# Moving weight conversions between steps: three doubled steps in the first feed-forward layer, two steps with none in the second

## The chip, the cores and the metric

One NeuronCore of a Trainium2 chip runs the whole program in one launch. The metric is the device time of that launch in microseconds (us). The engines are named as in the profile: PE multiplies matrices (PEld are its weight loads), DVE works elementwise, ACT evaluates functions and copies, POOL works elementwise too, and SP issues the DMAs.

## The reference

The program computes an attention with rotary embedding (2 batches, 8 heads, 576 positions, 64 per head) and passes its result, 1152 tokens of 512 features, through two feed-forward layers with 2048 hidden features:

```python
x = attention(q, k, v)                     # 1152 x 512
h = x @ moe_w_in;   g = where(h > 0, h, exp(min(h, 0)) - 1)       # first layer, ELU
x = g @ moe_w_out
h = x @ moe2_w_in;  g = h * tanh(softplus(h))                     # second layer, Mish
out = g @ moe2_w_out
```

The four weight matrices arrive as 64-bit floats, everything else as 32-bit floats.

## The kernel before, in words

**Products in three passes.** Every operand of a product is split into a high and a low part (`XH` and `XL` for activations entering a layer, two halves of a `g` tile for activations between the two products of a layer, and pairs such as `wi0h`, `wi0l` for weights), and the product is the sum high x high, high x low, low x high.

**Steps.** After attention the program is a sequence of 64 steps, numbered 0 to 63, one call of `step(n, late)` each. `half` is 32: steps 0 to 31 belong to the first layer, 32 to 63 to the second. A step first issues `g1_mm` (L199): 24 matmuls of 288 columns (L207) that make one 128 x 576 block of `h` in a PSUM tile `ps_s`, of which there are two until step 39. Then it issues the activation function of that block, and then one or two units of the second product that are due: in the first layer `g2_first` (24 matmuls of 288 columns, L752), in the second `g2_second` (12 matmuls of 512 columns, L781). Four of the first layer's second products are due only in steps 34, 35, 36 and 38; they complete the activations of batch 1 for the second layer, with `Y` added on DVE (L765), `XH` copied on ACT (L766) and `XL` subtracted on DVE (L767). The second layer's first product reads batch 1 from step 40 on.

**The activation functions.** In the first layer ACT runs L238, L239 and L240, DVE runs L241 and L242 (L242 is the last reader of `ps_s`), ACT copies the high part (L247) and DVE subtracts the low part (L251). In the second layer ACT reads `ps_s` twice (L708, L709; L709 is its last reader), DVE multiplies (L710), and for a batch of steps together ACT loads a table and runs L716, loads another and runs L722, after which DVE (L723, L730) and ACT (L729) finish the `g` tiles.

**Weight conversions.** There are 64 weight blocks ("jobs") of 128 x 512 numbers. `weight_stages` (L86) converts one from 64 to 32 bits and splits it: POOL multiplies (L96), DVE runs three operations (L100, L104, L108), ACT copies the high part (L125), POOL subtracts the low part (L128). Three buffers `raw` hold blocks that were loaded (L78, L83) and two buffers `wu` blocks under work. The generator yields between these, so that `advance(i)` does the next piece of the i-th of the two running jobs; `open_job` starts one (L96), `weight_part` opens jobs until two run and advances the first, `weight_job` calls it until one more job is done. Eight jobs are done during attention. Steps 4 to 30 do one job each: three pieces ahead of the activation function, the last piece (L125, L128) between L240 and L247. From step 31 on `weight_job` comes at the end of a step, once per step, and twice in step 36 (`XJ`). Jobs 40 to 43 are the blocks `wo0h`, `wo0l` that the first `g2_second` of step 39 multiplies with.

**Order.** In the first layer the order of every engine is the program's own. In the second layer (from step 32) that holds for ACT alone; the order on the other engines is chosen by the scheduler of the language from its own costs. Every engine works through its list in order.

Of the kernel before, what the change touches and what calls it, by code (L numbers as in the profile page):

```python
# [27 lines left out]
def kernel(  # L28
# [109 lines left out]
    def prefetch_weights():  # L138
        while loaded[0] < min(len(jobs), freed[0] + 3):
            load_weight(jobs[loaded[0]])  # L140
            loaded[0] += 1

    def open_job():
        prefetch_weights()
        running.append(weight_stages(jobs[opened[0]]))
        opened[0] += 1
        advance(-1)

    def advance(i):
        if next(running[i], True):  # L150
            running.pop(i)
            njob[0] += 1
# [21 lines left out]
    def weight_part():  # L174
        while len(running) < 2 and opened[0] < len(jobs):
            open_job()
        if running:
            advance(0)

    def weight_job():  # L180
        n = min(njob[0] + 1, len(jobs))
        while njob[0] < n:
            weight_part()
# [15 lines left out]
    def g1_mm(m, f, b):  # L199
        c = m * NF + f  # L200
        hi, lo = WI[c]
        o = ps_s()
        k = 0
        for cc in range(NC):
            for w, x in ((hi, XH), (hi, XL), (lo, XH)):
                for j in range(2):
                    nc.tensor.matmul(  # L207
                        o[:, j, :HS], lhsT=w[:, cc, :], rhs=x[:, b, cc, j * HS:j * HS + HS],
                        start=(k == 0), stop=(k == 3 * NC - 1),
                    )  # L210
                k += 1
        return o
# [22 lines left out]
    def elu(m, f, b, o):  # L235
        h = o[:, :, :HS]
        t, g = tmp("ta"), tmp("tb")
        nc.scalar.activation(out=v2(g), in_=h, func=AF.Relu, scale=-1.0)  # L238
        nc.scalar.activation(out=t, in_=g, func=AF.Exp, scale=-1.0)  # L239
        nc.scalar.activation(out=g, in_=g, func=AF.Tanh, scale=-0.5)  # L240
        nc.vector.scalar_tensor_tensor(out=g, in0=t, scalar=1.0, in1=g, op0=ALU.add, op1=ALU.mult)  # L241
        nc.vector.tensor_tensor(out=v2(g), in0=v2(g), in1=h, op=ALU.max)  # L242
        return m, f, b, g

    def elu_hi(m, f, b, g):
        gh, gl = galloc(m, f, b)
        nc.scalar.activation(out=gh, in_=g, func=AF.Copy)  # L247
        return g, gh, gl

    def elu_lo(g, gh, gl):  # L250
        nc.vector.tensor_tensor(out=gl, in0=g, in1=plain(gh), op=ALU.subtract)  # L251
# [438 lines left out]
    def moe(mp, early):  # L690
# [15 lines left out]
        def mish_a(n, m, f, b, o):  # L706
            t, s = tmp("ta"), tmp("tb")
            nc.scalar.activation(out=v2(t), in_=o[:, :, :HS], func=AF.Tanh, scale=0.5)  # L708
            nc.scalar.activation(out=v2(s), in_=o[:, :, :HS], func=AF.Silu)  # L709
            nc.vector.scalar_tensor_tensor(out=s, in0=t, scalar=-3.0, in1=s, op0=ALU.add, op1=ALU.mult)  # L710
            mst[n] = (m, f, b, t, s)

        def mish_b(ns):
            for n in ns:
                t = mst[n][3]
                nc.scalar.activation(out=t, in_=t, func=AF.Ln, scale=-NEAR_HALF, bias=half_col)  # L716

        def mish_c(ns):
            nc.scalar.preload_act_table_set("silu_and_others")
            for n in ns:  # L720
                m, f, b, t, s = mst[n]
                nc.scalar.activation(out=t, in_=t, func=AF.Tanh, scale=-1.0)  # L722
                nc.vector.scalar_tensor_tensor(out=s, in0=t, scalar=1.0, in1=s, op0=ALU.add, op1=ALU.mult)  # L723

        def mish_d(ns):
            for n in ns:
                m, f, b, t, s = mst.pop(n)
                gh, gl = galloc(m, f, b)
                nc.scalar.activation(out=gh, in_=s, func=AF.Copy, scale=-0.25)  # L729
                nc.vector.scalar_tensor_tensor(  # L730
                    out=gl, in0=s, scalar=-0.25, in1=plain(gh), op0=ALU.mult, op1=ALU.subtract
                )
                seam(m, f, b)
# [60 lines left out]
        blocks[-4:] = [(1, g, b) for g in range(NG - 2, NG) for b in range(NB)]  # L794
        g1_seq = [(m, g * GF + fi, b) for m, g, b in blocks for fi in range(GF)]
        half = len(g1_seq) // 2
        D1, D2, LATE, XJ = 1, 4, (3, 4, 5, 7), 4
        pend = []

        def run_g2(it):  # L800
            if it[0] == 0:
                g2_first(*it[1])
            else:
                g2_second(*it[1])
# [6 lines left out]
        def step(n, late):  # L811
            m, f, b = g1_seq[n]
            o = early.pop(n) if n in early else g1_mm(m, f, b)
            if late:
                mish_c(late)
            done, late = late, []
            if m == 0:
                for _ in range(3 if GF <= n < half - 1 else 0):
                    weight_part()
                if o is not None:  # L820
                    o = elu(m, f, b, o)
                if GF <= n < half - 1:
                    weight_part()
                if o is not None:
                    o = elu_hi(*o)
            else:
                mish_a(n, m, f, b, o)
                mish_d(done)
            if f % GF == GF - 1:
                g = f // GF  # L830
                if m == 0:
                    pend.extend((n + (D1 if n < half - 1 else LATE[e]), (0, (g, b, e))) for e in range(NC))
                else:
                    pend.extend((n + D2, (1, (g, t))) for t in TB[b])
            if n in batches:
                late = batches[n]
                mish_b(late)
            cnt = 2 if len(pend) > 5 or pend and pend[0][1][0] == 0 and n in (half - 2, half + 6) else 1
            while pend and cnt and pend[0][0] <= n:
                run_g2(pend.pop(0)[1])  # L840
                cnt -= 1
            if m == 0:
                if o is not None:
                    elu_lo(*o)
            for _ in range(0 if n < half - 1 else 1 + (n == half + XJ)):
                weight_job()
            return late

# [9 lines left out]
        with tc.manual_schedule():  # L858
            for n in range(half):
                step(n, [])  # L860
        with tc.manual_schedule(engines=MANUAL):
            late = []
            for n in range(half, 2 * half):
                if n == half + 7:
                    psum("ps_h")
                    s_more[0] = g_pool[0]
                    s_count[0] = 0
                late = step(n, late)
            mish_c(late)
            mish_d(late)  # L870
            while pend:
                run_g2(pend.pop(0)[1])
# [18 lines left out]
    with tc.tile_pool(name="mp", bufs=1, reuse_waits="tile") as mp:  # L891
        moe(mp, early)
# [54 lines left out]
```

## Time and profile before

| | us |
|---|---|
| median of 3 runs | 596.75 |
| lowest and highest of these | 593.58, 596.79 |
| the profiled execution's own time | 596.55 |
| its span in the trace | 594.8 |
| PE busy | 562.9 |
| DVE busy | 430.5 |
| ACT busy | 362.5 |
| POOL busy | 242.5 |

The span is what the trace covers; the execution's own time is 1.75 us longer. Busy times are sums over the whole span, so an engine with a small share can still be the one that is waited for in a short stretch. Times in rows are counted from the start of the span. In the rows, an entry in square brackets at the end gives the idle time of that engine just before the row and who ended it.

### The profile page before, as it was taken

How to read it: one execution, taken by the hardware profiler on the slowest of the kernel's cores; microseconds unless marked ns; L12 is line 12 of the kernel's file. 1: busy time of each engine (PE TensorE's matmuls, PEld its weight loads, DVE VectorE, ACT ScalarE, POOL GpSimd, SP SyncE). 2: the span in 40 equal slices, each digit the busy share in tenths (PEclk: the TensorE clock that was granted, in tenths of full speed). 3: DMA queues.
4: the chain of work that ended last, by engine and by line, in shares of the span. 5: the costliest groups of instructions: out<-in, count | busy, mean ns of one | idle time of the engine just before them, and what ended most of it. 6: DMA issues, size and time to landing. Idle time of an engine off the chain costs nothing.

```text
span 594.8 us, 10228 instructions
## 1 busy us (share of the span) xinstructions
PE 562.9 (95%) x3866; PEld 506.9 (85%) x3866; DVE 430.5 (72%) x650; ACT 362.5 (61%) x646; POOL 242.5 (41%) x214
## 2 busy tenths in 40 slices
PE   8879988989998999999999999996999999999997
PEld 8667666757778999999999999994899898999985
DVE  7688989788856766777777777887578667674452
ACT  3646756667765665555455465875776857568650
POOL 7759979771021323323323321555145243341000
PEclk9999999999999999999999999997899999999999
DMA  6267776744111323223222222324152241300022
GB/s 220 85 212 219 238 193 172 212 106 118 38 34 36 107 72 97 82 71 96 84 72 95 84 72 72 106 89 143 44 150 72 89 124 50 111 19 1 19 89 88
DMA packets 43121, 60.69 MB, mean 102 GB/s; under 512 B 13760, under 2 KB 31936, under 8 KB 42304
## 3 DMA queue, kind: packets, MB, share of 16 engines
q1 hardware_dynamic: 43072, 60.05, 33.4%
q8 instruction: 30, 0.49, 0.4%
q14 instruction: 19, 0.16, 0.1%
HBM read 46.20 MB, written 2.36 MB: 82 GB/s over the span
## 4 chain that ended last, share of the span: by engine, by line
PE 38%; issue 30%; DVE 16%; POOL 13%; ACT 2%; DMA 1%; SPq 0%; POOLq 0%; DVEq 0%; ACTq 0%
PE ps_h L781 17%; PE ps_s L207 13%; DVE mn L434 4%; POOL wu L96 4%; PE ps_s L425 3%; DVE pt L510 3%; PE psT L494 3%; POOL wi1l L128 3%; POOL wo0l L128 2%; POOL wo1l L128 2%; POOL wi0l L128 2%; DVE R L463 2%; DVE wu L104 2%; DVE wu L108 1%; ACT P L447 1%
## 5 line engine op out<-in xcount | busy, mean ns | idle before, releaser
L447 ACT ACTIVATE P<-ps_s,mn 128x576 f32<-128x576 f32 x72 | 52.9, 738 | 31.8 <-DVE mn L434 31.4
L494 PE MATMUL psT<-idn,P 128*128 128x128 f32 (+1 forms) x360 | 53.0, 278 | 16.4 <-DVE pt L510 16.2
L494 PEld LDWEIGHTS psT<-idn,P 128*128 128x128 f32 (+1 forms) x360 | 38.2, 134 | 32.9 <-DVE pt L510 30.0
L434 DVE TENSOR_REDUCE mn<-ps_s 128x1 f32<-128x576 f32 x72 | 51.8, 750 | 19.6 <-PE ps_s L425 19.1
L128 POOL TENSOR_TENSOR wo0l<-wu,wo0h 128x512 fp32r<-128x512 f32 x16 | 25.3, 1581 | 87.1 <-ACT wo0h L125 83.5
L100 DVE TENSOR_SCALAR wu<-wu 128x512 int32<-128x512 int32 x64 | 32.8, 513 | 35.2 <-POOL wu L96 35.2
L207 PE MATMUL ps_s<-XH,wi0h 128*128 128x288 f32 x256 | 55.2, 297 | 1.8 <-DVE tb L242 1.7
L207 PE MATMUL ps_s<-XH,wi1h 128*128 128x288 f32 x256 | 55.1, 296 | 1.4 <-ACT tb L709 1.4
L128 POOL TENSOR_TENSOR wi1l<-wu,wi1h 128x512 fp32r<-128x512 f32 x16 | 25.2, 1577 | 73.5 <-ACT wi1h L125 73.5
L207 PE MATMUL ps_s<-XH,wi1l 128*128 128x288 f32 x256 | 54.9, 295 | 0.0
L207 PE MATMUL ps_s<-XL,wi1h 128*128 128x288 f32 x256 | 54.8, 295 | 0.0
L207 PE MATMUL ps_s<-XL,wi0h 128*128 128x288 f32 x256 | 54.6, 295 | 0.0
L207 PE MATMUL ps_s<-XH,wi0l 128*128 128x288 f32 x256 | 54.6, 295 | 0.0
L104 DVE SCALAR_TENSOR_TENSOR wu<-raw,wu 128x512 int32<-128x512 int32 x64 | 50.1, 783 | 1.9
L96 POOL TENSOR_SCALAR wu<-raw 128x512 f32<-128x512 f32 x64 | 46.8, 732 | 11.3 <-DMA raw<-in_w_in_dram 6.1
L108 DVE SCALAR_TENSOR_TENSOR wu<-raw,wu 128x512 int32<-128x512 int32 x64 | 49.2, 769 | 1.6
L128 POOL TENSOR_TENSOR wo1l<-wu,wo1h 128x512 fp32r<-128x512 f32 x16 | 24.0, 1503 | 63.4 <-ACT wo1h L125 63.4
L241 DVE SCALAR_TENSOR_TENSOR tb<-ta,tb 128x576 f32<-128x576 f32 x30 | 23.1, 768 | 33.5 <-ACT tb L240 33.3
L238 ACT ACTIVATE tb<-ps_s 128x576 f32<-128x576 f32 x30 | 19.6, 653 | 44.7 <-PE ps_s L207 43.2
L518 PE MATMUL psA<-pt,v_t 128*64 128x256 f32 (+1 forms) x320 | 46.5, 417 | 0.0
L708 ACT ACTIVATE ta<-ps_s 128x576 f32<-128x576 f32 x32 | 20.6, 644 | 40.2 <-PE ps_s L207 40.2
L207 PEld LDWEIGHTS ps_s<-XH,wi0h 128*128 128x128 f32 x256 | 41.6, 189 | 3.6 <-DVE tb L242 2.3
(150 smaller groups left out, 1547.0 us busy)
## 6 DMA issues: line engine op xcount, KB each, us to landing
raw<-in_w_in_dram SPq DMA_DIRECT2D x32, 512.0 KB, 3.7
raw<-in_w_out_dram SPq DMA_DIRECT2D x32, 512.0 KB, 3.3
qk_t<-in_qk_dram SPq DMA_DIRECT2D x6, 1152.0 KB, 5.3
qa<-qh SPq DMA_DIRECT2D x24, 144.0 KB, 2.5
v_t<-in_vp_dram SPq DMA_DIRECT2D x8, 320.0 KB, 3.0
out_dram<-Y SPq DMA_DIRECT2D x9, 256.0 KB, 2.0
ka<-kh SPq DMA_DIRECT2D x12, 144.0 KB, 2.8
ka<-kl SPq DMA_DIRECT2D x12, 144.0 KB, 2.5
```

The source lines that it names most:

```text
L96: nc.gpsimd.tensor_scalar(out=u, in0=high.bitcast(F32), scalar1=REBASE, scalar2=0.0, op0=ALU.mult, op1=ALU.add)
L100: nc.vector.tensor_scalar(out=ui, in0=ui, scalar1=3, scalar2=0x7FFFFFF8, op0=ALU.logical_shift_left, op1=ALU.bitwise_and)
L104: nc.vector.scalar_tensor_tensor(out=ui, in0=high, scalar=-0x80000000, in1=ui, op0=ALU.bitwise_and, op1=ALU.bitwise_or)
L108: nc.vector.scalar_tensor_tensor(out=ui, in0=low, scalar=29, in1=ui, op0=ALU.logical_shift_right, op1=ALU.bitwise_or)
L128: nc.gpsimd.tensor_tensor(out=lo, in0=u, in1=plain(hi), op=ALU.subtract)
L207: nc.tensor.matmul(o[:, j, :HS], lhsT=w[:, cc, :], rhs=x[:, b, cc, j * HS:j * HS + HS], start=(k == 0), stop=(k == 3 * NC - 1),)
L241: nc.vector.scalar_tensor_tensor(out=g, in0=t, scalar=1.0, in1=g, op0=ALU.add, op1=ALU.mult)
L434: nc.vector.tensor_reduce(out=m, in_=psS[u][:, :, :HS], axis=AX.XY, op=ALU.min)
L447: nc.scalar.activation(out=P.rearrange("p (j n) -> p j n", j=2), in_=psS.pop(u)[:, :, :HS], func=AF.Exp, scale=-1.0, bias=mn_t.pop(u), acc ...
L494: nc.tensor.transpose(tv[:w, c, :], P[:, c * 128:c * 128 + w], idn)
L518: nc.tensor.matmul(o[64 * h:64 * h + 64, :n], lhsT=v_t[p][:, c, 64 * h:64 * h + 64], rhs=pt_t[p, g][:, h, c, :], start=(c == 0), stop=(c = ...
L781: nc.tensor.matmul(o, lhsT=l, rhs=w, start=(k == 0), stop=(k == 3 * GF - 1))
```

## The change

Steps 22, 25 and 28 (`TWICE`) now do two jobs instead of one: after the three pieces of the first running job come three pieces of the second (`advance(1)`), and after the last piece of the first the last piece of the second, after which two new jobs are opened. The second job of step 36 goes (`XJ` is gone), and steps 37 and 38 (`PAUSE`) do none. The number of jobs done is three higher after step 30, two higher after step 36, and equal from step 38 on.

```diff
-        D1, D2, LATE, XJ = 1, 4, (3, 4, 5, 7), 4
+        D1, D2, LATE = 1, 4, (3, 4, 5, 7)
+        TWICE, PAUSE = (half - 10, half - 7, half - 4), (half + 5, half + 6)
...
                 for _ in range(3 if GF <= n < half - 1 else 0):
                     weight_part()
+                for _ in range(3 if n in TWICE else 0):
+                    advance(1)
                 if o is not None:
                     o = elu(m, f, b, o)
                 if GF <= n < half - 1:
                     weight_part()
+                if n in TWICE:
+                    advance(0)
+                    open_job()
+                    open_job()
...
-            for _ in range(0 if n < half - 1 else 1 + (n == half + XJ)):
+            for _ in range(0 if n < half - 1 or n in PAUSE else 1):
                 weight_job()
```

PE's order is the same in both kernels. Three places on the other engines:

DVE in step 22, a doubled step. `wu` and `raw` are the buffers of a conversion, `tb` and `ta` those of the activation function. Before:

```order
L251 TENSOR_TENSOR g_3454<-tb_3444,g_3454 128x576
L100 TENSOR_SCALAR wu_3436<-wu_3436 128x512
L104 SCALAR_TENSOR_TENSOR wu_3436<-raw_3297,wu_3436 128x512
L108 SCALAR_TENSOR_TENSOR wu_3436<-raw_3297,wu_3436 128x512
L241 SCALAR_TENSOR_TENSOR tb_3516<-ta_3515,tb_3516 128x576
L242 TENSOR_TENSOR tb_3516<-tb_3516,ps_s_3483 128x576
```

Now:

```order
L251 TENSOR_TENSOR g_3454<-tb_3444,g_3454 128x576
L100 TENSOR_SCALAR wu_3436<-wu_3436 128x512
L104 SCALAR_TENSOR_TENSOR wu_3436<-raw_3297,wu_3436 128x512
L108 SCALAR_TENSOR_TENSOR wu_3436<-raw_3297,wu_3436 128x512
L100 TENSOR_SCALAR wu_3508<-wu_3508 128x512
L104 SCALAR_TENSOR_TENSOR wu_3508<-raw_3369,wu_3508 128x512
L108 SCALAR_TENSOR_TENSOR wu_3508<-raw_3369,wu_3508 128x512
L241 SCALAR_TENSOR_TENSOR tb_3521<-ta_3520,tb_3521 128x576
L242 TENSOR_TENSOR tb_3521<-tb_3521,ps_s_3483 128x576
```

Three more operations, of a second job, stand ahead of the activation function's L241.

ACT from the end of step 36 to step 39. The three pairs L708, L709 read the `ps_s` of steps 37, 38 and 39. Before:

```order
L766 ACTIVATE XH<-Y 128x576
L125 ACTIVATE wo0h<-wu 128x512 x2
L708 ACTIVATE ta<-ps_s 128x576
L709 ACTIVATE tb<-ps_s 128x576
L125 ACTIVATE wo0h<-wu 128x512
L708 ACTIVATE ta<-ps_s 128x576
L709 ACTIVATE tb<-ps_s 128x576
L766 ACTIVATE XH<-Y 128x576
L125 ACTIVATE wo0h<-wu 128x512
L708 ACTIVATE ta<-ps_s 128x576
L709 ACTIVATE tb<-ps_s 128x576
```

Now:

```order
L766 ACTIVATE XH<-Y 128x576
L125 ACTIVATE wo0h<-wu 128x512
L708 ACTIVATE ta<-ps_s 128x576
L709 ACTIVATE tb<-ps_s 128x576
L708 ACTIVATE ta<-ps_s 128x576
L709 ACTIVATE tb<-ps_s 128x576
L766 ACTIVATE XH<-Y 128x576
L708 ACTIVATE ta<-ps_s 128x576
L709 ACTIVATE tb<-ps_s 128x576
```

Three of the four copies of `wo0h` have left this stretch; they stand earlier in ACT's list. The remaining one is the last of the four.

DVE in step 35, where the scheduler's order differs. Before:

```order
L730 SCALAR_TENSOR_TENSOR g<-tb,g 128x576 x2
L767 TENSOR_TENSOR XL<-Y,XH 128x576
L108 SCALAR_TENSOR_TENSOR wu<-raw,wu 128x512
L710 SCALAR_TENSOR_TENSOR tb<-ta,tb 128x576
L765 TENSOR_TENSOR Y<-Y,ps_g 128x576
```

Now:

```order
L730 SCALAR_TENSOR_TENSOR g<-tb,g 128x576 x2
L767 TENSOR_TENSOR XL<-Y,XH 128x576
L108 SCALAR_TENSOR_TENSOR wu<-raw,wu 128x512
L765 TENSOR_TENSOR Y<-Y,ps_g 128x576
L710 SCALAR_TENSOR_TENSOR tb<-ta,tb 128x576
```

L765 and L710 have changed places.

## Rows read from the trace of the kernel before

**Rows 1.** The page, parts 1 and 2: PE's busy time; granted clock in 40 slices.

```profile
PE 562.9 (95%) x3866; PEld 506.9 (85%) x3866; DVE 430.5 (72%) x650; ACT 362.5 (61%) x646; POOL 242.5 (41%) x214
...
PEclk9999999999999999999999999997899999999999
```

**Rows 2.** Waits of PE, 180 to 595 us: waiter, awaited, total us, times, longest.

```profile
PE ps_h L781 <- ACT wo0h L125: 4.0, 1, 4.0
...
PE ps_s L207 <- ACT tb L709: 1.4, 1, 1.4
PE ps_h L781 <- POOL wo0l L128: 0.9, 2, 0.7
```

**Rows 3.** Windows: us, busy PE, PEld, DVE, ACT, POOL (x), granted clock, DMA, GB/s.

```profile
250.00:300.00 50.00, 50.00 (x379) 50.00 (x378) 37.61 (x56) 25.16 (x39) 15.83 (x16) 1.00 0.26 80
...
402.40:408.00 5.60, 5.33 (x33) 4.63 (x33) 5.51 (x6) 1.72 (x3) 3.40 (x4) 1.00 0.38 131
...
411.00:412.00 1.00, 0.00 (x0) 0.00 (x0) 0.96 (x3) 0.85 (x2) 0.00 (x0) 0.50 0.96 381
...
420.00:560.00 140.00, 140.00 (x832) 126.70 (x831) 96.42 (x142) 98.25 (x153) 48.70 (x38) 1.00 0.24 69
```

**Rows 4.** Timeline, PE, steps 38 to 41: start us, duration us, what, [idle before <-releaser].

```profile
394.22 0.54 PE L207 MATMUL ps_s<-XH,wi1h 128*128 128x288 f32 x2
...
402.32 0.53 PE L207 MATMUL ps_s<-XH,wi1h 128*128 128x288 f32 x2 [1.43 <-ACT tb L709]
...
407.91 0.50 PE L781 MATMUL ps_h<-wo0l,g 128*128 128x512 f32 x1 [0.27 <-POOL wo0l L128]
412.41 1.22 PE L781 MATMUL ps_h<-wo0h,g 128*128 128x512 f32 x2 [4.00 <-ACT wo0h L125]
414.30 0.79 PE L781 MATMUL ps_h<-wo0l,g 128*128 128x512 f32 x1 [0.67 <-POOL wo0l L128]
...
420.01 0.50 PE L207 MATMUL ps_s<-XH,wi0h 128*128 128x288 f32 x2
...
423.27 0.63 PE L781 MATMUL ps_h<-wo0h,g 128*128 128x512 f32 x2
...
428.87 0.42 PE L207 MATMUL ps_s<-XH,wi0h 128*128 128x288 f32 x2
```

**Rows 5.** Timeline, ACT, steps 36 to 39.

```profile
393.53 0.64 ACT L709 ACTIVATE tb<-ps_s 128x576 f32<-128x576 f32 x1
...
400.55 0.63 ACT L125 ACTIVATE wo0h<-wu 128x512 fp32r<-128x512 f32 x1 [2.07 <-DVE wu L108]
...
405.74 0.63 ACT L125 ACTIVATE wo0h<-wu 128x512 fp32r<-128x512 f32 x1 [3.48 <-DVE wu L108]
...
411.15 0.68 ACT L766 ACTIVATE XH<-Y 128x576 fp32r<-128x576 f32 x1 [3.69 <-DVE Y L765]
411.74 0.61 ACT L125 ACTIVATE wo0h<-wu 128x512 fp32r<-128x512 f32 x1
```

**Rows 6.** Timeline, DVE, a step of the first layer with a conversion (step 27).

```profile
335.40 0.41 DVE L100 TENSOR_SCALAR wu<-wu 128x512 int32<-128x512 int32 x1
...
336.57 0.69 DVE L108 SCALAR_TENSOR_TENSOR wu<-raw,wu 128x512 int32<-128x512 int32 x1
338.61 0.76 DVE L241 SCALAR_TENSOR_TENSOR tb<-ta,tb 128x576 f32<-128x576 f32 x1 [1.35 <-ACT tb L240]
```

**Rows 7.** Timeline, DVE, the last low part of batch 0, and step 35.

```profile
364.31 0.76 DVE L767 TENSOR_TENSOR XL<-Y,XH 128x576 fp32r<-128x576 f32 x1 [0.75 <-ACT XH L766]
...
387.57 0.74 DVE L710 SCALAR_TENSOR_TENSOR tb<-ta,tb 128x576 f32<-128x576 f32 x1
388.24 0.74 DVE L765 TENSOR_TENSOR Y<-Y,ps_g 128x576 f32<-128x576 f32 x1
```

**Rows 8.** Timeline, POOL: subtractions of low parts, in steps 35 and 38.

```profile
385.67 3.80 POOL L128 TENSOR_TENSOR wi1l<-wu,wi1h 128x512 fp32r<-128x512 f32 x1 [3.71 <-ACT wi1h L125]
...
402.35 1.29 POOL L128 TENSOR_TENSOR wo0l<-wu,wo0h 128x512 fp32r<-128x512 f32 x1
```

## The prediction, made before the changed kernel ran

> **What bounds the kernel now.** I began with the page: PE is busy for 562.9 of 594.8 us, and its granted clock is full in every slice but two, just past two thirds of the span [rows 1]. That names the engine to watch and one place where it loses time. The list of what PE waited for, from 180 us on, is short: 4.0 us once for ACT's copy of a high weight part, 1.4 us once for ACT's L709, 0.9 us twice for POOL's low part [rows 2]. The windows say how the rest looks. From 250 to 300 us PE is busy for all 50 us, so the first layer is bound by PE; from 420 to 560 us it is busy for all 140, so the rest of the second layer is too; between them the granted clock is 1.00 at 402.4 to 408 us and 0.50 at 411 to 412 us [rows 3], which are TensorE's levels of 2.4 and 1.2 GHz. The timeline of PE places all of this in steps 38 and 39: an idle 1.43 us ahead of step 39, then 0.27, 4.00 and 0.67 us inside the first `g2_second` [rows 4].
>
> Then I asked what ACT did ahead of these. Its L125 at 400.55 had waited 2.07 us for DVE's L108, the L125 at 405.74 3.48 us for the next L108, and the L766 at 411.15 3.69 us for L765 [rows 5]. Since ACT works in order, L708 and L709 of steps 37 and 38, whose PSUM blocks were long complete, stood behind the L125s. The fourth copy of `wo0h` stood behind L766, and L766 behind a DVE with three conversions in its list. It ends at 412.35, and PE's 4.00 us end at 412.41. So the conversions of steps 36 to 38 are themselves what PE waits for, directly or through the queue of ACT.
>
> **The sum, part by part.** The profiled execution took 596.55 us, 0.2 below the median of 596.75 and 3 above the lowest run.
>
> *The seam, gained.* From the start of step 38's first product to that of step 40 pass 420.01 - 394.22 = 25.8 us [rows 4]. PE's work there is 72 matmuls of 288 columns and 24 of 512. At full clock the former cost 50 us / 379 = 0.132 us each [rows 3], so 9.5 us; 24 of the latter take 428.87 - 423.27 = 5.6 us in step 40 [rows 4]. That is 15.1 us of work, and 10.7 us are lost: 1.43 + 0.27 + 4.00 + 0.67 = 6.4 of idle time, and 4.3 in matmuls at half clock and restarts. With the change no L125 stands between the L708 pairs of steps 37, 38 and 39, and the last copy of `wo0h` comes ahead of them all, where before the first two came. Before, the first of these two was done by 398.5 (2.07 idle us ahead of 400.55), so all four high parts should be there around then. The low part follows: 3.80 us for a subtraction at worst [rows 8] gives 402.3. Step 39's second product begins after two steps' work, at about 394.2 + 6.3 + 3.2 = 403.7 or later. Nothing it needs is late, so I take all 10.7 back. The ends: 6.4 if only the idle time goes and the clock falls all the same, 10.7 if all goes.
>
> *The seam, lost.* In step 35 the scheduler now puts L765 ahead of L710. L710 feeds L716 on ACT, and behind L716 in ACT's list stand L766, L125, a table load, L722 and then L708 and L709 of step 36. That L709 ended at 394.17 and step 38, which takes over its block, began at 394.22 [rows 5, 4], so a delay of L710 can delay PE one to one. The order alone shifts L710 by 388.24 - 387.57 = 0.67 us [rows 7]. Beside that there is POOL: its subtraction at 385.67 took 3.80 us, against 1.29 for the one at 402.35, and ended 1.23 us after L765 began [rows 8, 7]. So it ran only once DVE came to an operation that reads PSUM, and an operation like L710 that follows L765 finds it running with 1.29 - 0.67 = 0.6 us to go. I take half a microsecond of that: +1.1 us. The ends are 0 (if ACT comes to L716 that late anyway) and 0.67 + 1.29 = 2.0. An idle stretch of 1.3 us is like the 1.43 ahead of step 39, after which the granted clock stayed at 1.00 [rows 4, 3], so I charge no clock.
>
> *The doubled steps.* Each adds three DVE operations. The three in a row take 336.57 + 0.69 - 335.40 = 1.86 us, and DVE then idles 1.35 us for ACT's L240 [rows 6]. L241 and the release of `ps_s` are thus 0.5 us late in that step. The block's buffer is wanted again only two steps later, and the low part L251 only at the end of a group of four; steps 22, 25 and 28 are third, second and first in theirs. The next step's idle 1.35 us absorb the 0.5. Only behind step 28, where L765 and L767 fill DVE's idle time, may the 0.5 persist until the last low part of batch 0. That ended at 365.07 [rows 7], and step 32 wants it with its fourth quarter, 18 x 0.132 = 2.4 us into a product that began at about 365.0: 2.3 us of cover. ACT, busy for 25.16 of 50 us in this layer [rows 3], gets one more L125 of 0.63 us [rows 5], and the `raw` loads are 64 in both kernels, moved by at most two steps on SP. POOL does 2 x (1.3 + 0.66) us in 6.3. Cost: 0. Ends: 0 (no gain is possible where PE is busy for 50 of 50 us) and 3 x 0.5 = 1.5 if nothing absorbs it.
>
> *After step 40.* The jobs done are equal, PE's order is the same and PE is never idle until 560 us [rows 3], so what is gained arrives at the end.
>
> Sum: 596.55 - 10.7 + 1.1 + 0 = **587.0 us**, 1.6% below the median.
>
> **The rivals.** *A, the forecast:* 585.9 to 588.9 by the ends above, and up to 590 with a smaller part of the restarts. Chance 0.62.
>
> *B, half of it comes back.* The idle time ahead of step 38 grows toward 2 us or more and the granted clock falls there as it now does in the idle 4.00 us; that then costs what it costs now, 4.3 us. Or L709 of a later step finds itself behind L766 and its wait for L765 (3.69 us now [rows 5]). For it: L766 still stands between the pairs of steps 38 and 39. Against it: DVE has three conversions less in front of L765. Time: 587.0 + 4.3 = 591.3, with the higher delay of L710 592.2; to 593.5 with a second wait of 1.4. Chance 0.20.
>
> *C, no change.* The conversions are not what ends last: DVE and POOL are as late with mish and `XL` work as they are now, and the 4.00 us go to another tile. For it: DVE is busy for 5.51 of 5.60 us from 402.4 to 408 [rows 3]. Against it: of the DVE time there most is L100, L104 and L108, and the change takes them out. Time: 594 to 598. Chance 0.11.
>
> *D, slower.* The place is step 28, the mechanism POOL's subtraction beside a DVE that never pauses. In a doubled step two subtractions follow each other; if each takes 3.80 us as at 385.67 [rows 8] instead of 1.3, POOL needs 2 x (3.80 + 0.66) = 8.9 us in a step of 6.3, L100 of the next step comes some 4 to 5 us late, and DVE reaches the last L767 of batch 0 8 us late after three such steps. The cover of 2.3 us is gone, PE waits 5.7 us, the clock falls (4.3 us), and DVE enters the second layer behind, so that the seam keeps most of its loss: 596.55 + 5.7 + 4.3 - 4 = 602. It decides from the point where DVE has no gap for POOL. Against it: in the first layer DVE still pauses or reads PSUM in each step (L242, L762). The Trainium skill's page "SBUF — State Buffer", section "Who interferes with whom", speaks for D: a DVE operation with two SBUF inputs and a POOL operation that reads SBUF exclude each other, and the later one blocks fully. The stretched subtraction agrees with it; by that rule taken alone the doubled steps would cost as in D, by the pauses in DVE's list they cost nothing. Chance 0.07.
>
> **How the numbers follow.** About 1% is what a measurement of this kernel tells from no change, since its three runs span 0.5%. Faster by over 1% means below 590.8: A, and a small part of B, 0.65. Within 1%: the rest of B, and C, 0.28. Slower: D, 0.07. The range takes A and B: from 585.5 to 593.5; it leaves out C and D, 0.18. A's own range is 585.9 to 590.
>
> **What would show it.** Right: no row of PE waiting for L125 or L128 in steps 38 and 39; granted clock 1.00 in all slices but the last; about 16.5 us from step 38's first product to step 40's, with step 38 starting some 1 us late and an idle row for L709 there; PE busy throughout 250 to 365 us. Wrong: a granted clock of 0.50 anywhere between 380 and 430 us (B), an idle PE for L765 or L767 chains of the same length (C), subtractions above 3 us and L100 waiting for L96 in steps 23, 26 and 29 (D). The term I trust least is the 1.1 us in step 35.

## The result, and the profile after

The changed kernel takes 587.76 us in the median of 6 runs (587.66 to 589.50), the kernel before 596.14 in 6 (593.58 to 596.79). The ratio is 0.987 with a 95% interval of 0.985 to 0.989: 1.3% faster.

| us | before | after |
|---|---|---|
| median | 596.14 | 587.76 |
| the profiled execution's own time | 596.55 | 589.50 |
| its span | 594.8 | 587.7 |
| start of step 0 | 165.69 | 167.39 |
| start of step 32 | 364.99 | 366.66 |
| start of step 33 | 368.98 | 370.77 |
| start of step 35 | 378.12 | 379.92 |
| start of step 38 | 394.22 | 397.53 |
| start of step 40 | 420.01 | 412.82 |

The start of a step is that of its first product on PE. The profiled execution is the slowest of the six: it was already 1.70 us behind when step 0 began, after the attention that the two kernels share, and from step 0 to step 32, a stretch that holds the three doubled steps, both take 199.3 us. So the stages are compared, not the totals.

The page of the changed kernel, parts 1 and 2, which answer to [rows 1], gives PE's busy time and the granted clock by slices:

```profile
PE 558.7 (95%) x3866; PEld 504.2 (86%) x3866; DVE 431.3 (73%) x650; ACT 363.3 (62%) x646; POOL 244.5 (42%) x214
...
PEclk9999999999999999999999999999999999999999
```

PE is busy for 4.2 us less with the same 3866 matmuls, since none of them in the middle runs at half clock any more: no slice shows a drop. The list of PE's waits from 180 to 595 us, which answers to [rows 2], has two lines left:

```profile
PE ps_s L207 <- DVE tb L242: 1.9, 2, 1.7
PE ps_s L207 <- ACT tb L709: 1.5, 1, 1.5
```

The 1.7 us of the first line are there before, too, ahead of step 4 at 186 us; its other 0.2 us come ahead of step 33. Gone are the lines for L781. The windows answer to [rows 3] (us; then busy time of PE, PEld, DVE, ACT, POOL; granted clock; DMA):

```profile
250.00:365.00 115.00, 115.00 (x867) 115.00 (x866) 94.59 (x136) 61.53 (x95) 44.48 (x42) 1.00 0.31 97
...
397.00:413.00 16.00, 15.47 (x98) 14.40 (x99) 11.39 (x18) 9.23 (x15) 4.41 (x2) 1.00 0.25 75
413.00:560.00 147.00, 147.00 (x881) 133.26 (x881) 101.82 (x147) 107.33 (x167) 49.12 (x38) 1.00 0.22 65
```

PE never idles in the stretch that holds the doubled steps 22 to 28, nor from 413 to 560 us, and DVE is busy for 11.39 of 16 us in steps 38 and 39, where before it was busy for 5.51 of 5.60 us from 402.4 to 408 [rows 3]. PE's timeline of those steps, against [rows 4]:

```profile
397.53 0.53 PE L207 MATMUL ps_s<-XH,wi1h 128*128 128x288 f32 x2 [1.48 <-ACT tb L709]
...
407.23 0.63 PE L781 MATMUL ps_h<-wo0h,g 128*128 128x512 f32 x2
...
412.82 0.42 PE L207 MATMUL ps_s<-XH,wi0h 128*128 128x288 f32 x2
```

From step 38 to step 40 pass 15.29 us instead of 25.79; the three idle pieces ahead of L781 are gone, and its 24 matmuls in step 39 take 5.59 us. ACT's timeline of the same stretch, against [rows 5]:

```profile
396.84 0.64 ACT L709 ACTIVATE tb<-ps_s 128x576 f32<-128x576 f32 x1
...
400.44 0.62 ACT L125 ACTIVATE wo0h<-wu 128x512 fp32r<-128x512 f32 x1
...
401.49 0.64 ACT L709 ACTIVATE tb<-ps_s 128x576 f32<-128x576 f32 x1
...
402.55 0.66 ACT L709 ACTIVATE tb<-ps_s 128x576 f32<-128x576 f32 x1
408.92 0.69 ACT L766 ACTIVATE XH<-Y 128x576 fp32r<-128x576 f32 x1 [5.71 <-DVE Y L765]
```

The last `wo0h` is copied without a wait, 6.8 us ahead of the first L781, and the two L709 of steps 37 and 38 follow at once. L766 still waits for L765, longer than before, but nothing that PE needs stands behind it in time.

### The profile page after: what moved, and what is told of

Same layout as the page of the kernel before. It is cut to its first block, busy times and chain, and to the rows that moved or that the text cites. A ratio compares the mean times of both kernels' runs of the same rounds, so it can differ in the third digit from the quotient of the medians.

```text
span 587.7 us, 10232 instructions
## 1 busy us (share of the span) xinstructions
PE 558.7 (95%) x3866; PEld 504.2 (86%) x3866; DVE 431.3 (73%) x650; ACT 363.3 (62%) x646; POOL 244.5 (42%) x214
## 4 chain that ended last, share of the span: by engine, by line
PE 40%; issue 30%; DVE 15%; POOL 11%; ACT 3%; DMA 1%; SPq 0%; POOLq 0%; DVEq 0%; ACTq 0%
PE ps_h L781 17%; PE ps_s L207 14%; DVE mn L434 5%; POOL wu L96 4%; DVE pt L510 3%; PE ps_s L425 3%; PE psT L494 3%; POOL wi1l L128 2%; POOL wo0l L128 2%; DVE R L463 2%; POOL wi0l L128 2%; POOL wo1l L128 2%; ACT P L447 1%; PE psA L518 1%; DMA qk_t<-in_qk_dram 1%
## 5 line engine op out<-in xcount | busy, mean ns | idle before, releaser
L128 POOL TENSOR_TENSOR wo0l<-wu,wo0h 128x512 fp32r<-128x512 f32 x16 | 27.3, 1708 | 89.5 <-ACT wo0h L125 89.5
L100 DVE TENSOR_SCALAR wu<-wu 128x512 int32<-128x512 int32 x64 | 32.9, 513 | 35.5 <-POOL wu L96 35.5
L96 POOL TENSOR_SCALAR wu<-raw 128x512 f32<-128x512 f32 x64 | 48.6, 762 | 11.1 <-DMA raw<-in_w_in_dram 6.5
L104 DVE SCALAR_TENSOR_TENSOR wu<-raw,wu 128x512 int32<-128x512 int32 x64 | 49.3, 771 | 1.9
L128 POOL TENSOR_TENSOR wi1l<-wu,wi1h 128x512 fp32r<-128x512 f32 x16 | 23.0, 1441 | 66.7 <-ACT wi1h L125 66.7
L108 DVE SCALAR_TENSOR_TENSOR wu<-raw,wu 128x512 int32<-128x512 int32 x64 | 48.3, 755 | 1.6
L207 PEld LDWEIGHTS ps_s<-XH,wi1h 128*128 128x128 f32 x256 | 41.7, 188 | 2.3 <-ACT tb L709 1.7
L128 POOL TENSOR_TENSOR wi0l<-wu,wi0h 128x512 fp32r<-128x512 f32 x16 | 23.0, 1442 | 47.1 <-ACT wi0h L125 47.1
```

The costliest lines, as they stand in the source:

```text
L96: nc.gpsimd.tensor_scalar(out=u, in0=high.bitcast(F32), scalar1=REBASE, scalar2=0.0, op0=ALU.mult, op1=ALU.add)
L100: nc.vector.tensor_scalar(out=ui, in0=ui, scalar1=3, scalar2=0x7FFFFFF8, op0=ALU.logical_shift_left, op1=ALU.bitwise_and)
L104: nc.vector.scalar_tensor_tensor(out=ui, in0=high, scalar=-0x80000000, in1=ui, op0=ALU.bitwise_and, op1=ALU.bitwise_or)
L108: nc.vector.scalar_tensor_tensor(out=ui, in0=low, scalar=29, in1=ui, op0=ALU.logical_shift_right, op1=ALU.bitwise_or)
L128: nc.gpsimd.tensor_tensor(out=lo, in0=u, in1=plain(hi), op=ALU.subtract)
L207: nc.tensor.matmul(o[:, j, :HS], lhsT=w[:, cc, :], rhs=x[:, b, cc, j * HS:j * HS + HS], start=(k == 0), stop=(k == 3 * NC - 1),)
```

## The experiments

Eight kernels were run; times are medians, beside the kernel before at 596.45 us (15 runs with the first four) and 596.17 (25 runs with the other four). The kernel before differs by up to 0.3 us between the sets of runs, so a difference of that size between two sets says nothing.

| run | what differs | us (lowest to highest) |
|---|---|---|
| the change | doubled 22, 25, 28; none in 37, 38 | 587.76 (587.66 to 589.50) |
| e1 | as the change, but jobs in 37 and 38 | 589.38 (588.97 to 590.34) |
| e4 | doubled 19, 22, 25, 28; none in 35, 37, 38 | 586.09 (585.69 to 586.23) |
| e8 | doubled 19, 22, 25, 28; none in 36, 37, 38 | 586.25 (586.22 to 587.49) |
| e5 | as before, three copies on POOL | 594.75 (594.01 to 596.00) |
| e9 | as the change, ACT delayed in step 37 | 595.15 (594.22 to 595.97) |
| e3 | as the change, doubled 28, 29, 30 | 595.12 (594.05 to 596.44) |
| e2 | as the change, doubled 32, 33, 34 | 596.99 (595.63 to 597.87) |
| e7 | doubled 25, 28; none in 37 | 589.13 (588.83 to 589.51) |

**e1: the pauses undone.**

```diff
-        TWICE, PAUSE = (half - 10, half - 7, half - 4), (half + 5, half + 6)
+        TWICE, PAUSE = (half - 10, half - 7, half - 4), ()
```

> The three doubled steps and the single job in step 36 stay; steps 37 and 38 do one job each again (blocks of wo1, three steps ahead of before). Theory (an L125 of a late conversion in ACT's list holds L708 and L709 behind it): wo0 is early, so the waits of 4.0, 0.67 and 0.27 us in step 39 stay away; but the L125 of step 37 now has to wait until PE has read the old wo1h in step 38's second product, and L708 and L709 of step 38 stand behind it, so PE waits some 2 to 3 us at step 40: 590 to 592, and 594 if the granted clock falls there. Rival (the lead of three jobs is all that counts, the two pauses do nothing): 587.5 to 588.

589.38, 1.6 above the change and 0.6 under the theory's range: a wait behind ACT's queue, but smaller than the theory had it and at another operation. Its list of PE's waits:

```profile
PE ps_s L207 <- DVE tb L242: 1.9, 2, 1.7
PE ps_h L781 <- ACT Y L785: 1.7, 1, 1.7
PE ps_s L207 <- ACT tb L709: 1.4, 1, 1.4
```

and ACT's timeline around steps 37 to 40:

```profile
403.82 0.63 ACT L125 ACTIVATE wo1h<-wu 128x512 fp32r<-128x512 f32 x1 [2.62 <-DVE wu L108]
...
409.17 0.69 ACT L766 ACTIVATE XH<-Y 128x576 fp32r<-128x576 f32 x1 [3.63 <-DVE Y L765]
409.76 0.62 ACT L125 ACTIVATE wo1h<-wu 128x512 fp32r<-128x512 f32 x1
...
416.32 1.06 ACT L785 ACTIVATE Y<-ps_h 128x512 f32<-128x512 f32 x2
```

The L125 of step 37 waits again, though for DVE's L108 and not for PE's last use of the old block as I had said, and ACT comes later (one L716 ahead of L785 waits 0.76 us for DVE's L710), until L785 is late for the second product of step 40. So the lead of three jobs, with no second job in step 36, brings 7.1 of the 8.7 us that lie between the median of before in that set (596.45) and the change, and the pauses the rest.

**e4 and e8: a fourth doubled step, and no conversion in step 35, or in 36.**

```diff
-        TWICE, PAUSE = (half - 10, half - 7, half - 4), (half + 5, half + 6)
+        TWICE, PAUSE = (half - 13, half - 10, half - 7, half - 4), (half + 3, half + 5, half + 6)   # e4
+        TWICE, PAUSE = (half - 13, half - 10, half - 7, half - 4), (half + 4, half + 5, half + 6)   # e8
```

> A fourth doubled step (19) and a third step without a conversion (35). Theory (the idle 1.48 us ahead of step 38 in the changed kernel is L710 of step 35 behind L765 and POOL's subtraction, plus an L125 of 0.62 us in ACT's list): both are gone here, L710 stands ahead of L765 again, so that idle time goes and nothing else changes: 586.2 to 586.6 against 587.8 for the change. Rival (DVE as a whole is late in step 35 and 36, whatever stands in which place): the idle stays above 1 us, 587.5 to 588. Rival (a fourth doubled step costs what it brings): 588 or more.

> As the run with step 35 left out, but it is step 36 that does no conversion and step 35 does one (four doubled steps, steps 36, 37 and 38 without). L710 of step 35 stands ahead of L765 again, while the L125 in ACT's list of step 35 stays. Theory (the order of L710 and L765 is most of the 1.48 us): idle ahead of step 38 falls to 0.2 to 0.4 us, 586.5 to 586.9. Rival (the L125 in that place is most of it): the idle stays at 0.9 us or more, 587.2 to 587.8.

586.09 and 586.25, 0.1 and 0.25 under the theories' ranges: better than the change by 1.7 and 1.5 us, about the 1.48 us of idle time. In both traces the line for L709 is gone and one line of PE's waits is left; e4's:

```profile
PE ps_s L207 <- DVE tb L242: 1.9, 2, 1.7
```

DVE in step 35 of the change, and of e8, in that order:

```profile
390.06 0.75 DVE L765 TENSOR_TENSOR Y<-Y,ps_g 128x576 f32<-128x576 f32 x1
390.72 1.19 DVE L710 SCALAR_TENSOR_TENSOR tb<-ta,tb 128x576 f32<-128x576 f32 x1
```

```profile
387.92 0.75 DVE L710 SCALAR_TENSOR_TENSOR tb<-ta,tb 128x576 f32<-128x576 f32 x1
388.59 0.74 DVE L765 TENSOR_TENSOR Y<-Y,ps_g 128x576 f32<-128x576 f32 x1
```

With L710 second it comes later and takes 1.19 instead of 0.75 us. But this is not the only place where DVE's order differs, nor the first. DVE in step 34 and ACT's L729 behind it, in the kernel before and then in the change:

```profile
382.02 0.41 DVE L100 TENSOR_SCALAR wu<-wu 128x512 int32<-128x512 int32 x1
382.35 1.41 DVE L723 SCALAR_TENSOR_TENSOR tb<-ta,tb 128x576 f32<-128x576 f32 x2
383.13 1.36 ACT L729 ACTIVATE g<-tb 128x576 fp32r<-128x576 f32 x2
```

```profile
384.37 0.43 DVE L100 TENSOR_SCALAR wu<-wu 128x512 int32<-128x512 int32 x1 [1.27 <-POOL wu L96]
384.84 0.69 DVE L104 SCALAR_TENSOR_TENSOR wu<-raw,wu 128x512 int32<-128x512 int32 x1
385.44 1.42 DVE L723 SCALAR_TENSOR_TENSOR tb<-ta,tb 128x576 f32<-128x576 f32 x2
386.23 1.36 ACT L729 ACTIVATE g<-tb 128x576 fp32r<-128x576 f32 x2 [0.80 <-DVE tb L723]
```

In the change a conversion's L104 stands ahead of L723, behind an L100 that waits for POOL, and ACT's L729 waits for L723. Counted from the start of step 35, L729 begins after 6.31 us instead of 5.01, and from there to the L709 of step 36 ACT never stands still for more than 0.1 us. So ACT was 1.3 us late before it came to the operation that needs L710, and the wait for L710 added the last 0.2 of the 1.5. In e8 and e4 DVE runs L723 ahead of L104 again and L710 ahead of L765 again. They take both causes away together and do not divide the 1.5 us; the exchange of L710 and L765 alone was not run. e8 keeps step 35's L125 in ACT's list, so that the order on DVE, not the L125, made the wait. A fourth doubled step cost nothing. e4 is the fastest kernel of the study: its ratio to the kernel before is 0.9835 (0.981 to 0.986).

**e5: the kernel before, with three copies taken from ACT.**

```diff
-        nc.scalar.activation(out=hi, in_=u, func=AF.Copy)
+        if key in jobs[41:44]:
+            nc.gpsimd.tensor_scalar(out=hi, in0=u, scalar1=1.0, scalar2=0.0, op0=ALU.mult, op1=ALU.add)
+        else:
+            nc.scalar.activation(out=hi, in_=u, func=AF.Copy)
```

> The kernel before, with the high copy (L125) of jobs 41, 42 and 43, those of steps 36 and 37 and of the second job of 36, on POOL instead of ACT; L100, L104, L108 stay on DVE. Theory: two chains end late at the seam. ACT's queue gives the 1.43 us ahead of step 39, which goes; the 4.0 us are for data that DVE delivers late, and they stay or grow by the copy's time on POOL: 595 to 598, the granted clock still falls. Rival (ACT's order alone is the cause): the idle time and the half clock go, 587 to 589.

594.75, a ratio of 0.998 (0.996 to 0.999), 0.25 under the theory's range. Its lines for the seam (line numbers are three higher here):

```profile
PE ps_h L784 <- POOL wo0h L126: 3.5, 2, 2.7
...
PE ps_h L784 <- POOL wo0l L131: 0.7, 2, 0.5
```

The wait of step 39 for L709 has gone, so ACT's queue made that one; the wait for the high parts stays, and the granted clock falls again. The rival is out: taking the three copies from ACT's list is worth 1.7 us. It does not say that the 4.00 us were late data alone. In the kernel before, DVE's work on the fourth block of wo0 was this:

```profile
408.44 1.01 DVE L108 SCALAR_TENSOR_TENSOR wu<-raw,wu 128x512 int32<-128x512 int32 x1
```

The block was there at 409.45 and ACT stood idle, yet its copy began only at 411.74, behind L766 and its wait for L765 [rows 5]: 2.3 of the 4.00 us are ACT's order. In e5 POOL has three copies more to do, and the same L108 ends 16.3 us after the start of step 38 instead of 15.2, so the run moves the lateness as well as the queue.

**e9: an idle PE of known length.** The kernel computes the same; the copies write a spare tile.

```diff
             else:
+                for _ in range(14 if n == half + 5 else 0):
+                    nc.scalar.activation(out=spare, in_=spare, func=AF.Copy)
                 mish_a(n, m, f, b, o)
```

> The changed kernel with 14 spare copies of 128 x 288 on ACT in step 37, ahead of L708, dependent on each other, some 0.4 us each, about 5.6 us in all. They delay the release of the PSUM block that step 39 wants; some 1.9 us of that are covered. Theory (an idle PE of about 4 us costs a drop of the granted clock on top, some 3.5 to 4 us, as in the kernel before): 587.8 + 4 + 3.7 = 595 to 596, with a stretch at 0.50. Rival (the drop in the kernel before came from something else, such as the thin matmul work around it): the clock stays at 1.00 and the time is 591.5 to 592.5.

595.15: 7.4 us above the change for 4.53 us of idle time. PE's timeline (its L711 is the change's L709), and the windows of PE alone (busy time, granted clock, DMA):

```profile
406.82 0.85 PE L207 MATMUL ps_s<-XH,wi1h 128*128 128x288 f32 x2 [4.53 <-ACT tb L711]
```

```profile
395.00:402.00 7.00, 6.37 (x48) 1.00 0.11 29
402.00:407.00 5.00, 0.47 (x4) 0.78 0.47 142
407.00:410.00 3.00, 3.00 (x13) 0.50 0.32 112
410.00:412.00 2.00, 2.00 (x12) 0.60 0.00 0
412.00:420.00 8.00, 8.00 (x44) 1.00 0.01 2
```

The granted clock falls during the idle stretch and is back at full by 412. From step 38 to step 40 pass 22.19 us instead of the change's 15.29, 6.90 more: the 4.53 us, 2.2 in step 39 (11.01 against 8.79 us from its start to that of step 40), which is what the half clock costs, and 0.2 around the restart. The theory had 3.5 to 4 us for the clock. So an idle stretch of this length is enough for a drop, with nothing else of the kernel before; that the idle 4.00 us brought it there too is the likely reading, and the loss at the seam is larger than the idle time shown in the list of waits.

**e3 and e2: the doubled steps elsewhere.**

```diff
-        TWICE, PAUSE = (half - 10, half - 7, half - 4), (half + 5, half + 6)
+        TWICE, PAUSE = (half - 4, half - 3, half - 2), (half + 5, half + 6)                              # e3
+        TWICE, PAUSE, MORE = (), (half + 5, half + 6), (half, half + 1, half + 2)                        # e2
...
-            for _ in range(0 if n < half - 1 or n in PAUSE else 1):
+            for _ in range(0 if n < half - 1 or n in PAUSE else 1 + (n in MORE)):                        # e2
```

> The three doubled steps are 28, 29 and 30 instead of 22, 25 and 28; pauses as in the change. Theory (a doubled step is free because DVE's idle 1.35 us of the next step absorb its 0.5 us; from step 28 on there is no such idle time): DVE is late by 0.5 + 1.86 + 1.86 = 4.2 us at the last low part of batch 0, 2.3 us of that are covered, and PE waits about 2 us in step 32, perhaps more in 33: 589.5 to 591. Rival (the doubled steps are free wherever they stand, since PE works ahead): 587.5 to 588.2.

> No doubled step in the first layer; steps 32, 33 and 34 do two jobs each instead, and the pauses stay, so that wo0 is ready as early as in the change. Theory (what makes the change free is that the first layer's DVE and ACT have idle time and the first steps of the second have none): the added 1.86 us of DVE and 0.62 us of ACT per doubled step come out as idle PE in steps 34 to 38, 5 to 8 us in all and a drop of the granted clock if one idle stretch is long: 593 to 600. Rival (the two pauses are what counts, wherever the jobs go): 587.5 to 589.

595.12 and 596.99: in e3 nearly the whole gain is gone, in e2 all of it. In e3 PE's timeline shows what the theory named, the last parts of batch 0, but more of it, and further losses ahead of steps 36 and 38:

```profile
366.21 0.50 PE L207 MATMUL ps_s<-XH,wi0h 128*128 128x288 f32 x2 [1.00 <-DVE tb L242]
369.77 0.54 PE L207 MATMUL ps_s<-XL,wi0h 128*128 128x288 f32 x2 [1.46 <-DVE XL L767]
371.15 0.85 PE L207 MATMUL ps_s<-XH,wi0h 128*128 128x288 f32 x2 [0.58 <-ACT XH L766]
390.62 0.54 PE L207 MATMUL ps_s<-XH,wi1h 128*128 128x288 f32 x2 [0.83 <-ACT tb L709]
402.71 0.53 PE L207 MATMUL ps_s<-XH,wi1h 128*128 128x288 f32 x2 [2.24 <-ACT tb L709]
```

That is 6.1 us of idle time against 1.7 in the change, and the window after the first three has the granted clock at 0.51:

```profile
371.00:374.50 3.50, 3.35 (x13) 0.51 0.48 150
```

So the price that I had expected, 1.7 to 3.2 us above the change, was less than half of the 7.4 that it cost: I had not counted the lag that is carried into the second layer, nor the clock. The clock is the smaller part: the profiled execution of e3, with one drop, has a mean granted clock of 0.997, and four of the ten executions with a mean of 1.000 still took 594.05 to 594.70 us. And e3 changes two things, the spacing of the doubled steps and how near they stand to the last part of batch 0; it does not tell which of them counts. In e2 five waits for L709 add up to 5.9 us, the longest these, and the clock falls twice:

```profile
379.59 0.83 PE L207 MATMUL ps_s<-XH,wi0h 128*128 128x288 f32 x2 [1.87 <-ACT tb L709]
...
398.59 0.53 PE L207 MATMUL ps_s<-XH,wi1h 128*128 128x288 f32 x2 [2.56 <-ACT tb L709]
```

```profile
380.00:383.00 3.00, 3.00 (x14) 0.50 0.80 244
...
399.00:402.50 3.50, 3.50 (x20) 0.66 0.65 212
```

wo0 is ready in time there, and the two pauses stand; the gain is lost all the same. What makes the change pay is where the three jobs go.

**e7: one pause, two doubled steps.**

```diff
-        TWICE, PAUSE = (half - 10, half - 7, half - 4), (half + 5, half + 6)
+        TWICE, PAUSE = (half - 7, half - 4), (half + 5,)
```

> Two doubled steps (25, 28) and one pause (37): step 38 does the last job of wo0. Theory (its L125 stands behind L766, which waits for L765 on DVE until about 409, while PE wants that block at about 409.3 in step 39): PE waits about 1 us for the high part and 1 us for the low part: 589.3 to 590.5, no drop of the granted clock. Rival (the two pauses matter by the DVE time they free, half of it is half the gain): 591.5 to 592.5.

589.13, 1.4 above the change, and just under the expected range. PE's two new waits in step 39:

```profile
408.04 0.74 PE L781 MATMUL ps_h<-wo0h,g 128*128 128x512 f32 x2 [0.23 <-ACT wo0h L125]
409.44 0.50 PE L781 MATMUL ps_h<-wo0l,g 128*128 128x512 f32 x1 [0.67 <-POOL wo0l L128]
```

The last block is late in both parts as the theory had it, by 0.9 instead of 2 us. The gain does not follow the number of pauses: one pause and one doubled step less cost a sixth of it.

## Why the prediction was right, step by step

**The seam, gained: 10.7 us, measured 10.5** (25.79 - 15.29). The reading that the conversions of steps 36 to 38 are what PE waits for holds: with them out of the way all three waits go and so does the drop of the clock. e9 confirms the part that no list of waits shows, that idle time costs more than itself. e5 confirms that the 1.43 us were ACT's queue; of the 4.00 us, 2.3 were ACT's queue as well and the rest late data. One sign that I had given was wrong: I wrote 16.5 us for the interval from step 38 to step 40, but my own sum gives 15.1, as the idle time ahead of step 38 lies outside it.

**The seam, lost: 1.1 us, measured 1.5** (26.76 us from step 33 to step 38 against 25.24). This was the term that I trusted least, and here the number is better than the reason. L710 ends 1.80 us later than before, counted from the start of step 35: 0.67 for the order, as forecast, 0.44 for POOL, as forecast, and 0.7 by which DVE was late already, from step 34, which I had not seen. And ACT was 1.3 us late by itself, since L729 had waited for L723, so that undoing the exchange of L710 and L765 alone would have saved about 0.2 of the 1.5 us, an estimate from these rows. That the two delays run side by side and do not add up is luck for the forecast. POOL's subtraction beside L710 took 2.53 us:

```profile
388.77 2.53 POOL L128 TENSOR_TENSOR wo0l<-wu,wo0h 128x512 fp32r<-128x512 f32 x1 [4.43 <-ACT wo0h L125]
```

It ends at 391.30, and L710 at 391.91, 0.6 us after it. The Trainium skill's page "SBUF — State Buffer", section "Who interferes with whom", has a DVE operation with two SBUF inputs and a POOL operation that reads SBUF exclude each other. The 1.19 us of L710, whose inputs `ta` and `tb` both lie in SBUF, agree with it.

**The doubled steps: 0, measured 0.1** (4.11 us from step 32 to step 33 against 3.99; none up to step 32). I had the next step absorb the delay of 0.5 us; it takes one step more. Counted from the start of PE's step and against the usual 5.53 us, L241 is 0.4 us late in step 22 and 0.5 in step 23, where L100 waits 0.55 us for L96, a sign that I had given for rival D; in step 24 it is on time. So nothing passes on from steps 22 and 25. Behind step 28 it does: the last low part of batch 0, L767, starts 0.46 us after step 32 began, where before it started 0.68 us ahead of it [rows 7], so DVE is 1.1 us late and not 0.5, within the 2.3 us of cover. Step 33 then begins 0.1 us late behind L242. The two rows of POOL and DVE that speak to the slower rival:

```profile
347.25 2.96 POOL L128 TENSOR_TENSOR wi0l<-wu,wi0h 128x512 fp32r<-128x512 f32 x2 [4.31 <-ACT wi0h L125]
```

```profile
367.12 0.76 DVE L767 TENSOR_TENSOR XL<-Y,XH 128x576 fp32r<-128x576 f32 x1 [0.75 <-ACT XH L766]
```

Two subtractions in step 28 took 2.96 us together, not 7.6, so rival D had its place right and its price wrong. e3 is the case in which that place does become the bound: with the doubled steps one behind the other up to step 30 the change is worth 1 us.

**Rival B** did not come about, but it was nearer than I thought. I charged no clock for an idle 1.3 us because the 1.43 before had cost none; 1.48 in the change cost none either, while in e2 the clock fell at an idle 1.87 and in e3 after 1.00 and 1.46 in a row. But an idle 2.24 ahead of step 38 of e3 cost none: the granted clock was 1.00 from 402 to 409 us.

**After step 40** nothing changed: PE is busy throughout and what was gained arrived at the end. The total of 587.0 against 587.76 is off by 0.8 us: 0.2 in the first term, 0.4 in the second, 0.1 ahead of step 33 and 0.1 after step 40. Two sums that I had written beside it do not come out: the ends that I gave lead to 589.4 for A, and to 593.7 if only the idle time comes back, where I wrote 588.9 and 590; and D's sum is 602.6, not 602.

## What to carry to other kernels

Where a stage is bound by several engines in turn, work that is due there can be done ahead in a stage with one clear bound, but only where the lent engine can make up for the delay before its result is wanted: the same three jobs cost 0.1 us at steps 22, 25 and 28, 7 us at 28, 29 and 30, and the whole gain at 32 to 34. Read a short idle stretch of PE together with the granted clock behind it, and read each in-order engine's list for what stands behind a waiting instruction. And when a scheduler orders part of the program, compare its whole order after every such move: here DVE's order differed in step 34 as well as in step 35, that cost 1.5 us, and e4 and e8, with the old order, got it back. Follow such a delay back to the first operation that is late; the one that stands out need not be it.

## What the runs showed of the hardware

The granted clock can fall on less idle time than the 4.00 us of the kernel before: it did so at one idle stretch of 1.87 us in e2. It did not at 1.48 us in the change, nor at 2.24 us in e3, so the length of the stretch alone does not decide; what does these runs do not tell. Nor does a drop come in every execution of a kernel: in e3 the mean granted clock was 1.000 in four of ten executions, 0.997 in three (the profiled one, with one drop, is among these) and 0.994 in three.
